# Gated linear attention and a gated layer on one core: the SyncE queue's order, another queue for one transfer, and another way to count the verdict

## The chip, the cores and the metric

The kernel runs on one core of one Trainium2 chip. A core has TensorE (PE, matrix products; its weight loads are listed as PEld), VectorE (DVE), ScalarE (ACT), GpSimd (POOL) and SyncE (SP), and sixteen DMA engines [...]. The metric is the device time of one execution in microseconds, the median of several runs. Lower is better.

## What is computed

Two blocks follow each other. The first is a recurrence with a complex gate for each of 4 x 8 heads, 768 steps, head size 48; the second takes its output as 3072 rows of 384.

```python
mag = np.sqrt(a_re * a_re + a_im * a_im)
scale = np.minimum(mag, 0.999) / (mag + 1e-06)
a_re_n, a_im_n = (a_re * scale, a_im * scale)
for t in range(S):
    new_re = ar * S_re - ai * S_im
    new_im = ar * S_im + ai * S_re
    kv = np.einsum('bhd,bhe->bhde', k[:, :, t], v[:, :, t])
    S_re, S_im = (new_re + kv, new_im)
    y[:, :, t] = np.einsum('bhd,bhde->bhe', q[:, :, t], S_re)
...
x = y.transpose(0, 2, 1, 3).reshape(3072, 384)
h = x @ w_in            # 384 x 2048
g = h * np.cos(h)
out = g @ w_out         # 2048 x 384
```

## The kernel before

**Tiling.** The 768 steps of a batch are cut into 6 chunks of 128 steps, so there are 24 chunks; two chunks make a group, and there are 12 groups (g = 0 to 11). For a group the gates become logarithms and angles (`log_steps`), whose running sums over the chunk are products on PE (`p_powers` writes the PSUM tile `lgs`, `g_phase` writes `phs`). Such a sum is taken in two halves, `hi` (copied by ACT) and `lo` (the remainder, by DVE), each with its own product. Exponentials P, Q, sine and cosine then turn keys and queries into the stacks `ks` and `qs` (`g_stack`), so that the recurrence becomes an attention inside the chunk (scores `sc`, masked by DVE into `atm`, then `yp`) and a state that goes from chunk to chunk (`sp`, then `state` on DVE).

**Transposes.** From group 2 on `ks` and `qs` are transposed with the help of DRAM (`f_transpose`, lines 921 to 939): DVE transposes blocks of 32 x 32 into `tr`, one DMA writes `tr` to `moved`, and others read it back as `kT` (four DMAs with runs of 128 bytes) and as `qT` (one DMA with runs of 2 KB). The result `yT` of a group goes through DRAM as well: two DMAs write `x` (`f_x`), and one reads it back as `xT` (`f_xt`), which is what the second block multiplies. The last row of P goes out as `row` and comes back twice as `end` (`row_out`, `row_back`); `end` is scaled in `p_end` and used by the state.

**The second block.** For each group, eight blocks `hp` multiply `xT` by `w_in`; ACT and DVE make `gate` of each. The product with `w_out` is done with seven block products instead of eight (`seventh`, lines 1160 to 1202, into the PSUM tiles `sum` and `op`), after sums of quarters of `gate` (`mixed`). ACT and DVE move the parts to `ot`, and DMAs store `ot`.

**The verdict.** The fast path holds only for gates that are not extreme. Along the way minima and maxima are collected (`least`, `odd`, `wide`), at the end `verdict` (line 1608) makes a flag of them, all engines read it, and the program branches: the general path is run if the flag is set, and otherwise the last part of the output is stored by ACT's queue. With the inputs here the flag is not set. In the version before, two columns go to DRAM (`line_d`) and come back as one row, over which DVE takes the minimum. The weights arrive as 64-bit numbers and are fetched a second time in the loop to be looked at (`guard`, DMAs to `raw` on POOL's queue, each behind the copy `after`).

**Order.** Every product on PE is chained to the one before (`matmul`, line 686), so PE's order is the order in which the program is written. That order comes from `weave` (line 1213): each list of steps is spread evenly over a stretch of the iteration, step i of a list of m over lo to hi stands at lo + (hi - lo) (i + 0.5) / m, and all steps are run by that place. The loop over n = 2 to 11 (lines 1568 to 1576) weaves the chunks of group n, the seven products of group n - 1, the `hp` blocks of group n, and the gates of group n + 1. DVE, ACT and the DMA queues are ordered by a scheduler that works from the order of writing and its estimate of times, unless `behind` sets an instruction behind another. [...] Important lists here are `chunks(n)` over 0 to 0.36,

```python
for n in range(g * G, g * G + G):
    for hh in range(2):
        yield lambda n=n, hh=hh: f_scores(n, hh)
    yield lambda n=n: f_state(n)
    yield lambda n=n: f_out(n)
yield lambda: (f_x(g), f_xt(g))
if g + 2 < NG:
    yield lambda: load(g + 2, ("k", "q", "v"))
```

`prods(n + 1)` over 0.25 to 0.27 (its first two steps are the two `lgs` sums), `products(n - 1, 0, 3)` over 0 to 0.36, and `keys(n + 1)` after the middle. The last chunk of a batch has no state to pass on, and the first has none to take.

Of the kernel before, what the change touches and what calls it, by code (L numbers as in the profile page):

```python
# [11 lines left out]
F32 = mybir.dt.float32  # L12
# [7 lines left out]
ALU = mybir.AluOpType  # L20
# [467 lines left out]
def fast_path(ctx, tc, q, k, v, a_re, a_im, moe_w_in, moe_w_out, out, least, odd, wide,  # L488
# [323 lines left out]
    def even_steps(g, i, n):  # L812


        x = X[g]
        u = cut(x["mag"], i, n)
        P, Q = cut(x["P"], i, n), cut(x["Q"], i, n)
        ins = [vector.scalar_tensor_tensor(out=u, in0=Q, scalar=HUGE, in1=P,
                                           op0=ALU.min, op1=ALU.mult)]
        yield  # L820
        for t in P, Q:
            ins.append(vector.scalar_tensor_tensor(out=t, in0=u, scalar=3.0, in1=t,
                                                   op0=ALU.subtract, op1=ALU.mult))
            yield

        for one_, what in zip(ins, ("carried", "split")):
            if what in x and g > PEG:
                behind(one_, x[what])
        if g > 0:
            row_out(g, i, n, nc.sync)  # L830
            row_back(g, i, n, nc.sync)

    def row_out(g, i, n, queue):
        P = cut(X[g]["P"], i, n)
        queue.dma_start(out=X[g]["row"][ds(i * DM, n * DM)],
                        in_=P[C - 1:C].rearrange("o x -> (o x)"))

    def row_back(g, i, n, queue):
        row = X[g]["row"][ds(i * DM, n * DM)]
        end = X[g]["end"][:, ds(i * H, n * H)]  # L840
        for a in range(2):
            queue.dma_start(out=end[ds(a * D, D)], in_=row.rearrange("(x d) -> d x", d=D))

    def p_even(g, i, n):
        for _ in even_steps(g, i, n):
# [60 lines left out]
        special(out=sn, in_=ph, func=AF.Sin, scale=TWO_PI)  # L906
        special(out=cs, in_=cs, func=AF.Sin, scale=-TWO_PI, bias=half_pi_b)

    def g_stack(g, i, n):
        x = X[g]  # L910
        if i == 0:
            for name in "ks", "qs":
                x[name] = gt.tile([C, G * H, 2, D], F32, tag=name, name=name)
        for name, product in ("ks", "Q"), ("qs", "mag"):
            for a, trig in enumerate(("cos", "sin")):
                vector.tensor_tensor(
                    out=x[name][:, ds(i * H, n * H), a],
                    in0=cut(x[product], i, n).rearrange("p (x d) -> p x d", d=D),
                    in1=cut(x[trig], i, n).rearrange("p (x d) -> p x d", d=D), op=ALU.mult)

    def f_transpose(g, i, n, name):


        if i == 0:
            X[g][name] = ft.tile([D2, G * H, Q4, 32] if name == "kT" else [D2, Q4, G * H, 32], F32,
                                 tag=name, name=name, bufs=1)
        tr = ft.tile([C, NB, n * H, 32], F32, tag="tr", name="tr")
        turn = vector.transpose(out=tr, in_=X[g][name[0] + "s"][:, ds(i * H, n * H)].rearrange(
            "p x a d -> p x (a d)").rearrange("p x (r b) -> p b x r", b=NB))
        if name == "qT" and "gated" in X[g - 1]:  # L930
            behind(turn, X[g - 1]["gated"])
        moved = rows_d.tile([Q4, D2, n * H, 32], F32, tag="moved", name="moved", bufs=3)
        nc.sync.dma_start(out=moved.rearrange("q (r b) x j -> (q r) b x j", b=NB), in_=tr)
        if name == "kT":
            for q4 in range(Q4):
                nc.sync.dma_start(out=X[g][name][:, ds(i * H, n * H), q4], in_=moved[q4])
        else:
            nc.sync.dma_start(out=X[g][name][:, :, ds(i * H, n * H)],
                              in_=moved.rearrange("q c x j -> c q x j"))

    def f_turn(g, i, name, hh):

# [217 lines left out]
    def seventh(g, p, part):  # L1160


        x, name = X[g], SEVEN[p]
        if p == 0 and part == 0:
            x["sum"] = pm.tile([C, E2], F32, tag="acc", name="sum", bufs=1)
            x["ot"] = [msb.tile([C, DM], F32, tag="ot", name="ot") for _ in range(G)]

        alone = g == NG - 1 and p == 6
        summed = p in (0, 3, 5, 6) and not alone
        if not summed and part == 0:  # L1170
            x["op"] = pm.tile([C, E2], F32, tag="m", name="op", bufs=2)
        ps = x["sum"] if summed else x["op"]
        for j in range(part * HJ // 2, (part + 1) * HJ // 2):
            matmul(ps, lhsT=left(g, name, j), rhs=right[name][:, j],
                   start=(j == 0 and (p == 0 or not summed)),
                   stop=(j == HJ - 1), skip_group_check=summed)
        if part == 0:
            return
        c11, c12, c21, c22 = (x["ot"][i][:, ts(half, E2)] for i in range(2) for half in range(2))
        if g == NG - 1:  # L1180
            c12 = rest
        if p in (0, 3, 5) or p == 6 and not alone:
            late["scalar"] = scalar.mul(out={0: c11, 3: c21, 5: c22, 6: c12}[p], in_=ps, mul=scale)
        if g == NG - 1 and p == 5:
            scalar.mul(out=c12, in_=ps, mul=scale)
        for part_ in {1: [c11], 2: [c21], 4: [c21, c22], 6: [c12] * alone}.get(p, []):
            added = vector.scalar_tensor_tensor(out=part_, in0=ps, scalar=scale,
                                                in1=part_, op0=ALU.mult, op1=ALU.add)
            if alone:
                behind(added, late["read DVE"])  # L1190
            late["vector"] = added
        row = g * G * C
        if g == NG - 1 and p == 1:
            behind(nc.sync.dma_start(out=out[ds(row, C), 0:E2], in_=c11), late["line"])
        elif p == 4:
            put = nc.sync.dma_start(out=out[ds(row + C, C), :], in_=x["ot"][1])
            if g == NG - 1:
                behind(put, late["read SP"])
        elif p == 6 and alone:
            late["store"] = lambda: nc.scalar.dma_start(out=out[ds(row, C), E2:DM], in_=c12)  # L1200
        elif p == 6:
            nc.sync.dma_start(out=out[ds(row, C), :], in_=x["ot"][0])
# [23 lines left out]
    def keys(g):  # L1226

        if not 0 <= g < NG:
            return
        for i, n in spans(g):  # L1230
            yield lambda i=i, n=n: g_trig(g, i, n)
            yield lambda i=i, n=n: (g_stack(g, i, n), p_end(g, i, n))
            for name in "kT", "qT":
                if g >= PEG:
                    yield lambda i=i, n=n, name=name: f_transpose(g, i, n, name)

    def turned(g, i, name):
        return [lambda hh=hh: f_turn(g, i, name, hh) for hh in range(2)]
# [21 lines left out]
    def chunks(g):  # L1260
        for n in range(g * G, g * G + G):
# [1 line left out]
                yield lambda n=n, hh=hh: f_scores(n, hh)  # L1263
            yield lambda n=n: f_state(n)
            yield lambda n=n: f_out(n)
        yield lambda: (f_x(g), f_xt(g))
        if g + 2 < NG:
            yield lambda: load(g + 2, ("k", "q", "v"))

    def first(g):  # L1270
        order = range(NJ // 2) if g < PLAIN else (0, 4, 1, 5, 2, 6, 3, 7)
# [296 lines left out]
    for n in range(2, NG):  # L1568
        weave((mixes(n - 1, 2, 4), 0.0, 0.12), (logs(n + 1), 0.0, 0.02), (chunks(n), 0.0, 0.36),
              (upper[2:] if n == 2 else [], 0.0, 0.2), (products(n - 1, 0, 2 + (n < NG - 1)), 0.0, 0.36),  # L1570
              (prods(n + 1), 0.25, 0.27), (second(n - 1, 1), 0.36, 0.5),
              (products(n - 1, 2 + (n < NG - 1), 7), 0.4, 0.56),
              (phases(n + 1), *((0.472, 0.476) if n == PLAIN else (0.516, 0.524))),
              (keys(n + 1), *((0.5, 0.62) if n == PLAIN else (0.53, 0.64))),
              (last_quarter() if n == PLAIN else [], 0.9, 1.0), (first(n), 0.56, 1.0),
              (mixes(n, 0, 2), 0.9, 1.0), (guarded(n - 1, per) if n > 3 else [], 0.1, 0.9))
    checked = verdict(late, temp)

    def judged():
        late["tensor"] = tail["tensor"]  # L1580
        next(checked, None)

    weave((mixes(NG - 1, 2, 4), 0.0, 0.1), ([judged], 0.05, 0.15),
          (products(NG - 1, 0, 7), 0.0, 1.0), ([judged], 0.58, 0.6), ([judged], 0.76, 0.8))
    assert not guards
    return late
@with_exitstack
def kernel(ctx, tc, q, k, v, a_re, a_im, moe_w_in, moe_w_out, out):
# [16 lines left out]
        tc.add_manual_dep(ins.ins, other.ins.name, mybir.DependencyInfo(  # L1605
            mybir.DependencyClass.NoSync, mybir.DependencyReason.DATA))

    def verdict(late, temp):

        low = keep.tile([D2, 1], F32, name="low")  # L1610
        nc.vector.tensor_reduce(out=low, in_=least, axis=AX.X, op=ALU.min)
# [4 lines left out]
        nc.vector.tensor_scalar(out=even, in0=even, scalar1=0.0, scalar2=None, op0=ALU.is_le)  # L1616
        nc.vector.tensor_scalar(out=most, in0=most, scalar1=2.4, scalar2=None, op0=ALU.is_le)
        nc.vector.tensor_tensor(out=even, in0=even, in1=most, op=ALU.mult)
        line_d = scratch.tile([D2 + C], F32, name="line_d")
        behind(nc.sync.dma_start(out=line_d[0:D2], in_=low.rearrange("p o -> (p o)")),  # L1620
               late["x"])
        nc.sync.dma_start(out=line_d[D2:D2 + C], in_=even.rearrange("p o -> (p o)"))
        line = temp("Q")[0:1, 0:D2 + C]
        late["line"] = nc.sync.dma_start(out=line, in_=line_d.unsqueeze(0))
        yield
        bad = keep.tile([1, 2], F32, name="bad")
        behind(nc.vector.tensor_reduce(out=bad[:, 0:1], in_=line, axis=AX.X, op=ALU.min),
               late["vector"])
        flag = keep.tile([1, 1], I32, name="flag")
        nc.vector.tensor_scalar(out=flag, in0=bad[:, 0:1], scalar1=0.5, scalar2=None,  # L1630
                                op0=ALU.is_lt)
        reads, values = nc.values_load_multi_w_load_instructions(
            flag[0:1, 0:1], min_val=0, max_val=1,
            skip_runtime_bounds_check_because="a comparison gives 0 or 1")
# [43 lines left out]
```

## Time and profile before

| | us |
|---|---|
| median of 3 runs | 655.68 (655.22 to 656.19) |
| the profiled execution | 653.01 |
| its span, from first to last instruction | 651.2 |
| start to the loop over n (`hp` of group 2 begins) | 154.01 |
| `hp` of group 11 begins | 607.62 |
| end of the last PE product | 646.55 |
| SP: waits for x to be written, before `xT` | 7.6 in 11 |
| DVE: `rest`, the last addition | 646.64 to 647.00 |
| the DMAs of `raw`, 768 KB each, from issue to landing | 4.6 to 5.1 |
| all DMA | 94.90 MB, 232920 packets, of which 208701 under 512 bytes |

The profile is of one execution. Its page gives the busy time of each engine and the same in 40 slices of the span; the chain that ended last is followed back from the last instruction to whatever released it. A row of the view of waits names the instruction that waited, what released it, and then the sum, the number and the longest of these waits. A row of the timeline begins with start and length in us, then engine, source line, operation, output and inputs, shape and count; what follows in brackets is how long the engine was idle before it, and for whom. One product of float32 shows as two instructions in it. Since nearly all calls go through a few helpers, the line is often a helper's (687 is `matmul`, 676 the calls on DVE and ACT), and an instruction is known by its tile.

### The profile page before, as it was taken

Reading aid. Unit: us, or ns where it says so; the run is one execution under the profiler, and the core shown is the slowest. Engines: PE = TensorE matmul, PEld = TensorE weight load, DVE = VectorE, ACT = ScalarE, POOL = GpSimd, SP = SyncE. Lnnn points to the kernel's source line nnn. Section 1 sums busy time; section 2 is a strip of 40 time slices with the busy share of each in tenths; the row PEclk is TensorE's granted clock in tenths of the full one; section 3 lists DMA queues with packets and bytes.
Section 4 is the critical chain, followed back from the end, with each engine's and each line's share of the span. In section 5 each row is a group of like instructions: output and inputs, shape, how many; then the busy total and the mean of one; then the engine's idle time right before and its main releaser. Section 6 shows DMA issues by size and latency. Waiting matters only on the chain.

```text
span 651.2 us, 10758 instructions
## 1 busy us (share of the span) xinstructions
PE 641.0 (98%) x4075; PEld 576.4 (89%) x4075; DVE 492.0 (76%) x799; ACT 392.8 (60%) x726; POOL 30.9 (5%) x53
## 2 busy tenths in 40 slices
PE   8999999999999999999999999999999999999997
PEld 6888877777999999899899899899899999999996
DVE  6999989888687688786787787876877878862251
ACT  7898687284583593494494485485576476433330
POOL 4010200000000000010010010000000000000000
PEclk9999999999999999999999999999999999999999
DMA  9968755727627656747738737836836843363001
GB/s 249 244 179 203 225 164 123 170 62 182 146 49 182 158 146 148 194 110 167 209 82 191 204 85 167 205 96 151 226 105 146 219 123 98 112 134 120 25 1 31
DMA packets 232920, 94.90 MB, mean 146 GB/s; under 512 B 208701, under 2 KB 221246, under 8 KB 232858
## 3 DMA queue, kind: packets, MB, share of 16 engines
q1 hardware_dynamic: 225320, 68.51, 45.3%
q0 software_dynamic: 5824, 25.50, 11.7%
q8 instruction: 34, 0.56, 0.4%
q10 hardware_dynamic: 1714, 0.11, 0.2%
q14 instruction: 28, 0.23, 0.1%
HBM read 69.28 MB, written 24.81 MB: 144 GB/s over the span
## 4 chain that ended last, share of the span: by engine, by line
PE 92%; ACT 4%; DVE 3%; DMA 0%; issue 0%; SPq 0%; DVEq 0%
PE hp L687 38%; PE op L687 18%; PE sum L687 16%; PE sc L687 6%; PE yp L687 6%; PE sp L687 4%; PE phs L687 2%; PE lgs L687 1%; ACT tan L707 1%; PE yr L687 1%; PE tp L948 1%; ACT rs L707 1%; ACT lg L707 1%; ACT L703 1%; DVE mag L676 1%; DVE atm L676 1%
## 5 line engine op out<-in xcount | busy, mean ns | idle before, releaser
L687 PE MATMUL hp<-xT,w_in 128*128 128x256 f32 (+1 forms) x1176 | 252.5, 375 | 0.0
L687 PEld LDWEIGHTS hp<-xT,w_in 128*128 128x128 f32 x1176 | 219.6, 190 | 30.2 <-issue 0.2
L707 ACT ACTIVATE gate<-hp,half_pi_b 128x512 f32<-128x512 f32 x96 | 66.0, 687 | 118.5 <-PE hp L687 118.5
L687 PE MATMUL op<-w_out,gate 128*128 128x192 f32 (+1 forms) x448 | 100.7, 374 | 0.0
L676 DVE TENSOR_TENSOR gate<-hp,gate 128x512 f32<-128x512 f32 x96 | 65.7, 684 | 45.8 <-ACT junk L676 45.7
L687 PEld LDWEIGHTS op<-w_out,gate 128*128 128x128 f32 x448 | 75.9, 190 | 16.9 <-issue 2.0
L676 ACT ACTIVATE junk<-hp 128x512 bf16<-128x512 f32 x96 | 56.7, 591 | 0.0
L687 PE MATMUL sum<-t_s,s 128*128 128x192 f32 x320 | 56.3, 329 | 0.0
L687 PEld LDWEIGHTS sum<-t_s,s 128*128 128x128 f32 x320 | 52.1, 190 | 1.5 <-issue 1.5
L676 DVE TENSOR_TENSOR atm<-sc,causal 128x512 f32<-128x512 f32 x48 | 32.9, 689 | 23.4 <-PE sc L687 23.4
L687 PEld LDWEIGHTS sc<-qT,kT 96*128 96x128 f32 x384 | 47.4, 192 | 2.3 <-issue 0.6
L687 PE MATMUL sc<-qT,kT 96*128 96x128 f32 x384 | 49.0, 276 | 0.2 <-ACT qT L676 0.2
L676 ACT ACTIVATE ot<-sum 128x192 f32<-128x192 f32 x39 | 12.6, 322 | 53.7 <-PE sum L687 53.4
L676 DVE SCALAR_TENSOR_TENSOR ot<-op,ot 128x192 f32<-128x192 f32 x40 | 13.3, 354 | 38.0 <-PE op L687 36.4
L687 PE MATMUL yp<-atm,v 128*48 128x128 f32 x352 | 33.6, 277 | 0.9 <-ACT Q L707 0.6
L703 ACT ACT_TABLE_LOAD x24 | 30.8, 1283 | 1.2 <-PEq L1662 0.7
L676 ACT COPY yT<-yp 48x512 f32<-48x512 f32 x44 | 25.3, 574 | 7.4 <-PE yp L687 7.0
L687 PE MATMUL yp<-qT,state 96*48 96x128 f32 x304 | 29.7, 272 | 0.0
L687 PE MATMUL sum<-w_out,gate 128*128 128x192 f32 x160 | 29.7, 329 | 0.0
L687 PE MATMUL sp<-v,ks 128*96 128x48 f32 x320 | 29.7, 245 | 0.0
L687 PEld LDWEIGHTS sp<-v,ks 128*96 128x96 f32 x320 | 29.6, 165 | 0.0
L676 ACT CAST tan<-phs 128x384 int32<-128x384 f32 x24 | 11.4, 480 | 29.4 <-PE phs L687 29.4
(147 smaller groups left out, 987.4 us busy)
## 6 DMA issues: line engine op xcount, KB each, us to landing
moved<-tr SPq DMA_DIRECT2D x20, 768.0 KB
raw<-in_moe_w_in_dram POOLq DMA_DIRECT2D x16, 768.0 KB, 5.1
raw<-in_moe_w_out_dram POOLq DMA_DIRECT2D x16, 768.0 KB, 4.6
kT<-moved SPq DMA_DIRECT2D x40, 192.0 KB
qT<-moved SPq DMA_DIRECT2D x10, 768.0 KB
k<-in_k_dram SPq DMA_DIRECT2D x24, 192.0 KB
q<-in_q_dram SPq DMA_DIRECT2D x24, 192.0 KB
v<-in_v_dram SPq DMA_DIRECT2D x24, 192.0 KB
```

The lines of the kernel that those rows point to most:

```text
L676: ins = getattr(self.engine, op)(**kw)
L687: chain(nc.tensor.matmul(out, **kw), "tensor")
L703: chain(nc.scalar.preload_act_table_set(table))
L707: chain(nc.scalar.activation(func=func, **kw))
L948: chain(nc.tensor.transpose(ps[:, h], X[g][name[0] + "s"][:, x0 + h].rearrange("p a d -> p (a d)"), ident), "tensor")
```

## The change

From group 3 on, SP's DMAs around `xT` are put in one order by hand (`there_and_back`, `in_line`): x, row, xT, the two of end, then k, q and v of the group after next, then the store of the finished chunk. The steps for xT and the loads leave the list of `chunks(n)`, and `there_and_back(n)` is woven in at 0.36. `qT` from group 3 on is read back over POOL's queue, in a chain with the fetches of `raw`, whose stretch ends at 0.68 instead of 0.9. The stack of keys is made, then transposed, then the stack of queries; `p_end` comes after both. In the last group two scalings of a PSUM tile go from ACT to DVE. The verdict is multiplied into one column, which one product with a column of ones sums on PE; the flag compares that sum with 127.5.

```diff
-        if g > 0:
+        if 0 < g <= PLAIN + 1:
             row_out(g, i, n, nc.sync)
             row_back(g, i, n, nc.sync)
+    def in_line(**kw):
+        put = nc.sync.dma_start(**kw)
+        behind(put, late["x"])
+        late["x"] = put
+
+    def there_and_back(g):
+        if g + 1 < NG:
+            row_out(g + 1, 0, G, in_line)
+        f_xt(g)
+        if g + 1 < NG:
+            row_back(g + 1, 0, G, in_line)
+        if g + 2 < NG:
+            load(g + 2, ("k", "q", "v"), put=in_line)
...
-    def g_stack(g, i, n):
+    def g_stack(g, i, n, names=("ks", "qs")):
...
-            nc.sync.dma_start(out=X[g][name][:, :, ds(i * H, n * H)],
-                              in_=moved.rearrange("q c x j -> c q x j"))
+            queue = nc.sync if g <= PEG else nc.gpsimd
+            put = queue.dma_start(out=X[g][name][:, :, ds(i * H, n * H)],
+                                  in_=moved.rearrange("q c x j -> c q x j"))
+            if g > PEG:
+                chain(put, "gpsimd")
...
-        if p in (0, 3, 5) or p == 6 and not alone:
+        if g == NG - 1 and p == 5:
+            for out_ in c22, c12:
+                vector.tensor_scalar(out=out_, in0=ps, scalar1=scale, scalar2=None, op0=ALU.mult)
+        elif p in (0, 3, 5) or p == 6 and not alone:
             late["scalar"] = scalar.mul(out={0: c11, 3: c21, 5: c22, 6: c12}[p], in_=ps, mul=scale)
-        if g == NG - 1 and p == 5:
-            scalar.mul(out=c12, in_=ps, mul=scale)
...
-            behind(nc.sync.dma_start(out=out[ds(row, C), 0:E2], in_=c11), late["line"])
+            nc.sync.dma_start(out=out[ds(row, C), 0:E2], in_=c11)
         elif p == 4:
             put = nc.sync.dma_start(out=out[ds(row + C, C), :], in_=x["ot"][1])
-            if g == NG - 1:
-                behind(put, late["read SP"])
+            behind(put, late["read SP"] if g == NG - 1 else late["x"])
...
-            yield lambda i=i, n=n: (g_stack(g, i, n), p_end(g, i, n))
+            if g <= PEG:
+                yield lambda i=i, n=n: (g_stack(g, i, n), p_end(g, i, n))
             for name in "kT", "qT":
+                if g > PEG:
+                    yield lambda i=i, n=n, name=name: g_stack(g, i, n, (name[0] + "s",))
                 if g >= PEG:
                     yield lambda i=i, n=n, name=name: f_transpose(g, i, n, name)
+            if g > PEG:
+                yield lambda i=i, n=n: p_end(g, i, n)
...
-        yield lambda: (f_x(g), f_xt(g))
-        if g + 2 < NG:
-            yield lambda: load(g + 2, ("k", "q", "v"))
+        yield lambda: f_x(g)
+        if g == PLAIN:
+            yield lambda: (f_xt(g), load(g + 2, ("k", "q", "v")))
...
-              (prods(n + 1), 0.25, 0.27), (second(n - 1, 1), 0.36, 0.5),
+              (prods(n + 1), 0.25, 0.27),
+              ([lambda: there_and_back(n)] if n > PLAIN else [], 0.36, 0.37), (second(n - 1, 1), 0.36, 0.5),
...
-              (mixes(n, 0, 2), 0.9, 1.0), (guarded(n - 1, per) if n > 3 else [], 0.1, 0.9))
-    checked = verdict(late, temp)
+              (mixes(n, 0, 2), 0.9, 1.0), (guarded(n - 1, per) if n > 3 else [], 0.1, 0.68))
+    def counted(even):
+        ps = pa.tile([1, 1], F32, tag="a", name="good")
+        matmul(ps, lhsT=even, rhs=one_b, start=True, stop=True)
+        return ps
+
+    checked = verdict(late, counted)
...
-          (products(NG - 1, 0, 7), 0.0, 1.0), ([judged], 0.58, 0.6), ([judged], 0.76, 0.8))
+          (products(NG - 1, 0, 7), 0.0, 1.0), ([judged], 0.42, 0.44), ([judged], 0.76, 0.8))
...
-        line_d = scratch.tile([D2 + C], F32, name="line_d")
-        behind(nc.sync.dma_start(out=line_d[0:D2], in_=low.rearrange("p o -> (p o)")),
-               late["x"])
-        nc.sync.dma_start(out=line_d[D2:D2 + C], in_=even.rearrange("p o -> (p o)"))
-        line = temp("Q")[0:1, 0:D2 + C]
-        late["line"] = nc.sync.dma_start(out=line, in_=line_d.unsqueeze(0))
+        nc.vector.tensor_tensor(out=even[0:D2], in0=even[0:D2], in1=low, op=ALU.mult)
         yield
-        bad = keep.tile([1, 2], F32, name="bad")
-        behind(nc.vector.tensor_reduce(out=bad[:, 0:1], in_=line, axis=AX.X, op=ALU.min),
-               late["vector"])
+        good = counted(even)
         flag = keep.tile([1, 1], I32, name="flag")
-        nc.vector.tensor_scalar(out=flag, in0=bad[:, 0:1], scalar1=0.5, scalar2=None,
-                                op0=ALU.is_lt)
+        behind(nc.vector.tensor_scalar(out=flag, in0=good, scalar1=C - 0.5, scalar2=None,
+                                       op0=ALU.is_lt), late["vector"])
```

More of the change, by code (lines that the diff above doesn't have):

```diff
@@ L828, in even_steps @@
                 behind(one_, x[what])
-        if g > 0:
+        if 0 < g <= PLAIN + 1:
             row_out(g, i, n, nc.sync)
             row_back(g, i, n, nc.sync)
+    def in_line(**kw):
[10 more added lines that the diff above has]
+            load(g + 2, ("k", "q", "v"), put=in_line)
     def row_out(g, i, n, queue):
         P = cut(X[g]["P"], i, n)
-        queue.dma_start(out=X[g]["row"][ds(i * DM, n * DM)],
-                        in_=P[C - 1:C].rearrange("o x -> (o x)"))
+        getattr(queue, "dma_start", queue)(out=X[g]["row"][ds(i * DM, n * DM)],
+                                           in_=P[C - 1:C].rearrange("o x -> (o x)"))
     def row_back(g, i, n, queue):
@@ L841, in row_back @@
         for a in range(2):
-            queue.dma_start(out=end[ds(a * D, D)], in_=row.rearrange("(x d) -> d x", d=D))
+            getattr(queue, "dma_start", queue)(out=end[ds(a * D, D)], in_=row.rearrange("(x d) -> d x", d=D))
     def p_even(g, i, n):
@@ L907, in g_trig @@
         special(out=cs, in_=cs, func=AF.Sin, scale=-TWO_PI, bias=half_pi_b)
-    def g_stack(g, i, n):
+    def g_stack(g, i, n, names=("ks", "qs")):
         x = X[g]
-        if i == 0:
-            for name in "ks", "qs":
+        for name in names:
+            product = {"ks": "Q", "qs": "mag"}[name]
+            if i == 0:
                 x[name] = gt.tile([C, G * H, 2, D], F32, tag=name, name=name)
-        for name, product in ("ks", "Q"), ("qs", "mag"):
             for a, trig in enumerate(("cos", "sin")):
@@ L1606, in behind, with verdict @@
             mybir.DependencyClass.NoSync, mybir.DependencyReason.DATA))
-    def verdict(late, temp):
+    def verdict(late, counted):
         low = keep.tile([D2, 1], F32, name="low")
```

## The prediction

> **What bounds the kernel.** I read the page first: which engine is full, and in which slices it is not.
>
> ```profile
> span 651.2 us, 10758 instructions
> PE 641.0 (98%) x4075; PEld 576.4 (89%) x4075; DVE 492.0 (76%) x799; ACT 392.8 (60%) x726; POOL 30.9 (5%) x53
> ...
> PE   8999999999999999999999999999999999999997
> ...
> DMA  9968755727627656747738737836836843363001
> ```
>
> PE is full in every slice but the first and the last, so a transfer, or work of DVE or ACT, is worth time only where PE waits for it. The view of waits says where that is. Its rows give who waited for whom, the sum in us, the times and the longest; of PE's weight loads (PEld) in the loop:
>
> ```profile
> PEld yp L687 <- issue: 2.5, 11, 0.2
> ...
> PEld op L687 <- issue: 2.0, 11, 0.2
> ...
> PEld lgs L687 <- DVE lo L676: 1.6, 4, 0.5
> ...
> PEld sum L687 <- issue: 1.5, 8, 0.2
> ```
>
> No row has PE waiting for a DMA: all that SyncE (SP) brings is there in time in this execution. The one wait for data inside the loop is that of the log sums (lgs) for lo, a DVE result. I then took the period of the loop from the chain that ended last, between the blocks "20.72 PE hp L687 x96", which begin at 154.01, 204.33, 255.53, 305.77, 356.09, 407.30, 457.54, 507.86, 559.54 and 607.62. The periods repeat with the three kinds of chunk pair: A (first of a batch; n = 3, 6, 9) 50.32, B (n = 4, 7) 51.2, C (last of a batch; n = 5, 8) 50.24. One breaks the pattern: n = 10 is of kind B and takes 51.68, 0.47 more. Its timeline beside that of n = 7 is the key to this forecast. First n = 7:
>
> ```profile
> 385.82 1.95 PE L687 MATMUL sc<-qT,kT 96*128 96x128 f32 x16
> ...
> 388.39 0.95 DVE L676 SCALAR_TENSOR_TENSOR lo<-lg,hi 128x768 fp32r<-128x768 f32 x1
> ...
> 388.91 1.48 PE L687 MATMUL sp<-v,ks 128*96 128x48 f32 x16
> ...
> 390.47 0.34 PE L687 MATMUL lgs<-lo,exact 128*128 128x384 f32 x1
> ```
>
> then n = 10:
>
> ```profile
> 537.65 1.06 PE L687 MATMUL sc<-qT,kT 96*128 96x128 f32 x8
> ...
> 540.22 0.95 DVE L676 SCALAR_TENSOR_TENSOR lo<-lg,hi 128x768 fp32r<-128x768 f32 x1
> ...
> 541.22 0.19 PEld L687 LDWEIGHTS lgs<-lo,exact 128*128 128x128 f32 x1 [0.40 <-DVE lo L676]
> ...
> 541.86 1.48 PE L687 MATMUL sp<-v,ks 128*96 128x48 f32 x16
> ```
>
> At n = 7 the sixteen state products sp stand before lgs and cover DVE's way to lo. At n = 10 they stand behind it, and PE waits 0.40.
>
> [...] at n = 10 mag and lo follow the mask product atm, which waited 0.59 for PE. [...]
>
> **The change, part by part.**
>
> SP's order. SP now issues two x, row, xT, two end, k, q, v, stores; before, row at 398.55, x 398.88, end 399.79, one k 401.21, xT 402.08, then the rest. The instructions and bytes are the same; x no longer waits behind row (31.5 us over 11 such waits of SP on DVE lg), and xT has one 192 KB load less ahead of it. PE needs xT at 407.14 in this iteration and does not wait for it. Worth 0; work of the products before it covers it. Were the cover gone, each microsecond late would cost one. Row and end now stand behind x's wait for yT; end is needed only by p_end at 410.19, end's issue was over by 401.1, and x's input yT, copied by 395.71 before, is an estimated 2 us later now (one more sum block of 1.3 and a part of the wait below ahead of it), so about 398, as before. Cost 0.
>
> qT over POOL, nine times. SP is freed of 1.19 us each (its median issue), POOL is charged 0.72 to 0.77, as for raw, of which it has 95% free. POOL's order is raw, raw, qT, after. The second raw went out at 441.18, the next qT is due near 466, and after (430.38) comes later: nothing holds it. The trace doesn't show qT's landing on POOL. From below: raw, with as many bytes, lands 4.6 to 5.1 us after issue; moved is written by about 418.3 (traffic follows the transpose's end at 415.34), so 424, with sc due at 427.64. [...] I take 0, and keep up to 1 us an iteration as the bad end (the SP form ended near 426.2, and 528.0 at n = 10, so it gains at best 0.1).
>
> Split stacks. The same four products of 0.95 and two transposes of 2.25; the transpose of ks starts one product earlier, the first gate product (412.50) has the same work ahead of it, and hp's third buffer leaves 1.7 us (first buffer free 413.17, wanted 414.9). Cost 0.
>
> Verdict. Three DMAs and a reduction (0.38) go; one DVE product of 0.15 and a 1x1 product on PE come, with its weight load 0.1 to 0.2: +0.15. It needs even, ready at 632.05, and stands near 636. The removed round trip was over with flag at 642.27, while the end hangs on the last PE product, rest at 646.64 and the final store: no gain. The two scalings that move from ACT to DVE (0.33, 0.32) land in DVE gaps of 1.7 us and more: 0.
>
> The unasked part: the weave. chunks(n) loses its tenth item, the load. Ten items over 0 to 0.36 stood 0.036 apart, nine stand 0.04 apart. The second state product (index 6) was at 6.5 x 0.036 = 0.234, before the log sums at 0.252; now it is at 0.26, behind them. So n = 3 to 9 get the PE order of n = 10, which never had the load. PE is chained by hand, so this order is certain. Prices:
> - B, n = 4 and 7: DVE's order is that of n = 10 too. 0.40 each: 0.8.
> - C, n = 5 and 8: no second state product, and lgs waited 0.45 already. 0.
> - A, n = 3, 6, 9: here DVE's new order is atm, ot, mag, lo, with ot (0.35) ahead. ot waits for the op block that PE runs 0.89 to 2.36 after sc (as 538.54 to 540.01 against 537.65). At n = 6 sc begins at 334.61: op ends 336.97, ot ends 337.36, mag 338.2, lo 339.1. PE is ready for lo at about 3.3 after sc, 337.9: a wait of 1.2. Or from n = 10: lo comes 1.02 later than there, 0.40 + 1.02 = 1.42. I take 1.3 each: 3.9, kept between 1.15 and 1.42. ACT's hi shifts by one yT copy (0.58) to 337.76 and is not last.
>
> Sum: 3.9 + 0.8 + 0.15 = +4.85 (4.3 to 5.3). PE has no slack after lgs to take it back. Profiled execution: 653.01 (span 651.2 and 1.8 around) becomes 657.9. The median of the runs is 655.68, 2.67 above the profiled one; I add to that: **660.5**.
>
> **Rivals.**
> 1. *Relief.* The 2.67 may be late transfers in unprofiled runs, which the new SP order mends. For it: qT's traffic ends 1.4 before use. Against: no PE wait on DMA. Time: 655.68 - 2.67 + 4.85 = 657.9.
> 2. *Not slower: late xT at the hand-over.* The same mechanism, but larger: if unprofiled runs lose more than 4.85 / 9 = 0.54 us at each of nine hand-overs from yT to xT, the new order outweighs the waits. At 0.7 each: 655.68 - 6.3 + 4.85 = 654.2. It needs more than the 2.67 that can be seen between the executions.
> 3. *lo in time.* If the new DVE order costs nothing because lo's inputs come earlier, only the product remains: 655.8. Against: n = 10, where lo wasn't in time.
> 4. *qT late on POOL.* 1 us in nine iterations: 669.5 with the waits.
>
> **How the numbers follow.** Forecast 0.58 (own range 659.9 to 661.2), relief 0.18, not slower 0.15, lo in time 0.05, qT late 0.04. Forecast, relief and a part of the rest make 0.8: 656.6 to 662.0. A measurement of this kernel can tell about 0.2%, 1.3 us, from no change. Slower by more: forecast, relief and late qT, 0.80, less 0.03 for relief beyond what I grant it: 0.77. Within: 0.07. Faster: 0.16.
>
> **What would show it.** In the changed profile, the row of weight loads of lgs waiting for DVE lo should grow from 1.6 in 4 to about 6.3 in 9 (3.9 and 0.8 new, 0.9 at C, 0.4 at n = 10, 0.3 at the start), with 1.1 to 1.4 at n = 3, 6, 9; the periods A and B should read 51.6 and 51.6, C 50.2; the tail from the last hp block the same to 0.2. A new PE wait of sc for qT, or of hp for xT, would speak for rival 4 or a failed queue; periods of 50.3 and 51.2 with a smaller gap to the median would refute me.

## The result, and the profile after

The changed kernel takes 664.57 us on the median of 4 runs (664.14 to 664.94), the kernel before 655.93 beside it (655.22 to 656.41): ratio 1.0136, 95% interval 1.0121 to 1.0151, so it is 8.6 us slower. The profiled execution is 664.25 us, with a span of 662.4. That span is 11.2 more than in the profile of before, whose execution lay 2.67 below its median; the trace therefore shows more loss than the medians do.

First the page of the changed kernel: span, busy time of the engines, and the part on DMA queues (packets, MB, time of the packets as a share of 16 engines' span).

```profile
span 662.4 us, 10764 instructions
PE 644.2 (97%) x4077; PEld 576.4 (87%) x4077; DVE 493.2 (74%) x801; ACT 392.6 (59%) x724; POOL 40.3 (6%) x62
...
q1 hardware_dynamic: 221462, 61.43, 48.8%
q0 software_dynamic: 7696, 32.57, 16.9%
```

The same part of the page of before:

```profile
q1 hardware_dynamic: 225320, 68.51, 45.3%
q0 software_dynamic: 5824, 25.50, 11.7%
```

q1 is SyncE's queue, q0 GpSimd's. qT's 7.1 MB have gone from one to the other, as they should. But the two shares together went from 57.0 to 65.7%, for the same 94.9 MB and 1% fewer packets, over a longer span. Moving the same bytes took more packets' time than before. Nothing in the diff asks for that, and it turned out to be the key.

The view of waits of the changed kernel, weight loads (PEld) and then products (PE):

```profile
PEld lgs L687 <- DVE lo L676: 5.7, 9, 1.1
PEld sc L687 <- issue: 4.7, 9, 1.6
PEld sc L687 <- DMA qT<-moved: 3.7, 3, 1.9
```

```profile
PE sc L687 <- DMA kT<-moved: 3.8, 4, 1.6
PE lgs L687 <- DVE lo L676: 2.8, 4, 0.9
```

The first row is the wait that was forecast (1.6 in 4 before). The next rows for sc are new: the first scores of an iteration wait for kT or qT. Before, no row had sc waiting for a DMA; its longest row was this:

```profile
PEld sc L687 <- issue: 0.6, 3, 0.3
```

("issue" in the PEld row only says that the profile names no releaser; the same waits have one in the view of the products.) The timeline at n = 3 shows the forecast wait itself:

```profile
185.92 0.83 ACT L728 ACTIVATE hi<-lg 128x768 fp32r<-128x768 f32 x1
...
187.13 0.95 DVE L676 SCALAR_TENSOR_TENSOR lo<-lg,hi 128x768 fp32r<-128x768 f32 x1
...
188.13 0.19 PEld L687 LDWEIGHTS lgs<-lo,exact 128*128 128x128 f32 x1 [1.15 <-DVE lo L676]
...
188.59 0.51 PEld L687 LDWEIGHTS sp<-v,ks 128*96 128x96 f32 x4
```

The second state product sp, which used to stand ahead of lgs, now stands behind it.

The two losses can be told apart by iteration. The table is worked out from the traces: time from the first scores of iteration n to the start of its hp block, and from there to the first scores of n + 1 (20.72 when PE waits for nothing).

| n | 3 | 4 | 5 | 6 | 7 | 8 | 9 | 10 |
|---|---|---|---|---|---|---|---|---|
| scores to hp, before | 29.60 | 30.49 | 29.52 | 29.60 | 30.49 | 29.51 | 29.60 | 30.90 |
| scores to hp, after | 30.96 | 30.88 | 29.54 | 30.99 | 30.92 | 29.53 | 30.98 | 30.91 |
| hp to scores, before | 20.72 | 20.72 | 20.72 | 20.72 | 20.72 | 20.72 | 20.79 | 20.72 |
| hp to scores, after | 20.72 | 22.45 | 21.39 | 20.93 | 21.62 | 20.77 | 22.17 | 21.38 |

The upper pair is the weave: 1.36, 1.39 and 1.38 at n = 3, 6, 9, 0.39 and 0.43 at n = 4, 7, nothing at n = 5, 8, 10; together 4.95 us. The lower pair is the hand-over of kT and qT: 5.6 us that nobody had asked for, with another 0.8 up to the scores of n = 2.

### The profile page after: what moved, and what is told of

It is laid out like the page before. It is cut to its first block, busy times and chain, and to the rows that moved or that the text cites. A ratio compares the mean times of both kernels' runs of the same rounds, so it can differ in the third digit from the quotient of the medians.

```text
span 662.4 us, 10764 instructions
## 1 busy us (share of the span) xinstructions
PE 644.2 (97%) x4077; PEld 576.4 (87%) x4077; DVE 493.2 (74%) x801; ACT 392.6 (59%) x724; POOL 40.3 (6%) x62
## 4 chain that ended last, share of the span: by engine, by line
PE 76%; DVE 9%; DMA 7%; ACT 4%; SPq 3%; issue 2%; POOL 0%; DVEq 0%
PE hp L687 25%; PE op L687 17%; PE sum L687 14%; PE yp L687 5%; PE sc L687 5%; DMA kT<-moved 5%; PE sp L687 4%; SPq L951 3%; DVE tr L676 2%; PE phs L687 2%; PE lgs L687 1%; DVE mag L676 1%; DVE lo L676 1%; DVE ks L676 1%; DVE tan L676 1%
## 5 line engine op out<-in xcount | busy, mean ns | idle before, releaser
L687 PE MATMUL sum<-t_s,s 128*128 128x192 f32 x320 | 57.8, 330 | 0.0
L687 PE MATMUL sc<-qT,kT 96*128 96x128 f32 x384 | 50.8, 277 | 4.9 <-DMA kT<-moved 3.8
```

What stands on the lines that cost most here:

```text
L687: chain(nc.tensor.matmul(out, **kw), "tensor")
```

## The experiments

Theories at the start: *weave* (lgs ahead of sp) and *queue* (qT on GpSimd's queue and kT on SyncE's hold each other up, and both come late); against *queue*, that SyncE's new order, or the split stacks, make kT late. Runs marked "in before", and the four that take one part of the change each, edit the kernel before; the others edit the changed one. All times below are medians, and each ratio is the one found with its interval from the runs side by side, not the quotient of the medians; in the four series the kernel before took 654.66, 654.67, 654.49 and 655.33 beside them.

### Undoing the weave, the queue, both; and the queue alone

```
 def chunks(g):                      # e1_order, e3_both
     if g == PLAIN: ...
+    elif g + 2 < NG:
+        yield lambda: None
 def f_transpose(...)                # e2_qt_sync, e3_both: after; e4_before_pool: the reverse, in before
-    queue = nc.sync if g <= PEG else nc.gpsimd
+    queue = nc.sync
```

> The changed kernel with one empty tenth item put back into chunks(n) for n = 3 to 9, so that TensorE's order in the loop is that of the kernel before (the second state product ahead of the log sums again); queues, split stacks and verdict stay changed. Before 655.9, after 664.6 on the median. Two causes (the order of the weave, and qT that lands late for the scores from GpSimd's queue): the waits of lgs for lo shrink from 5.7 in 9 to about 1.6 in 4 in the row of weight loads, the waits of the scores for kT and qT stay: 660.3 (659.5 to 661.2). Order alone (the late scores are only a sequel of it): 656.0. Order worth nothing, the new SP sequence or qT's queue is all: 664.5.

> The changed kernel with qT written from SyncE's queue again, all else changed, the order of the weave too. Two causes: the scores' waits for kT and qT (8 in the sum of PE's weight loads and products over the iterations) go, those of lgs stay: 659.8 (658 to 660.8), near the forecast of 660.5. Rival, SyncE's new order (k, q, v loads and stores moved behind xT) makes moved and kT late whoever issues qT: no gain, 664 to 665. Order alone: 664.5 too, since the late scores would remain.

> The changed kernel with both undone: the empty tenth item in chunks and qT from SyncE's queue. What is left of the change is SyncE's new order, the split stacks, and the verdict by a product. Two causes: 655.5 (654 to 656.3), with no waits of lgs at n = 3 to 9 apart from C's 0.4 and no waits of the scores for kT or qT. If the hand-over from yT to xT gained something in unprofiled runs, below 654.5. Rival, SyncE's new order makes kT late: 659 to 661.

> The kernel before with nothing but qT written from GpSimd's queue for groups 3 to 11; SyncE's order, stacks, weave and verdict as before. Two causes: the scores wait for kT and qT as in the changed kernel, 4 to 5 in the median: 660.2 (658.5 to 661.5). Rival, SyncE's new order is what makes them late: 655.7 (655 to 656.5). Rival, only the order and the queue together do it (less time is left between stack and scores): 656 to 658.

| run | us | ratio to before | packets' time of the two queues |
|---|---|---|---|
| e1_order | 660.36 | 1.0085 (1.0067 to 1.0104) | 48.6 + 17.0% |
| e2_qt_sync | 663.75 | 1.0138 (1.0122 to 1.0155) | 54.1 + 11.8% |
| e3_both | 657.25 | 1.0039 (1.0024 to 1.0055) | 53.9 + 11.9% |
| e4_before_pool | 664.40 | 1.0167 (1.0140 to 1.0194) | 41.0 + 15.3% |

The first met its number for two causes, though the second cause will turn out to be another than the queue. The second run missed its number: with qT back on SyncE nothing was gained. Its trace holds a new wait, of the sums for ACT:

```profile
PE sum L687 <- ACT ot L676: 4.7, 4, 1.7
```

With qT on SyncE the scheduler places ACT's copies to ot and DVE's gate products otherwise, so this run changed more than a queue and can't price it. The third, with both undone, was expected at 655.5 and was still 2.6 slower than before: a third cause. The fourth, expected at 660.2, lost more than *queue* alone could explain. Two things stood out. The packets' time is near 66% in every version of the changed kernel, whichever queue carries qT, and below 57% in the fourth, so the queue doesn't set it. And in the fourth, GpSimd's queue held a second transfer right behind qT (timeline):

```profile
268.11 0.69 POOL L939 DMA_DIRECT2D qT<-moved  x1 [38.81 <-DMA moved<-tr]
...
268.80 0.76 POOL L629 DMA_DIRECT2D raw<-in_moe_w_in_dram  x1
```

In the changed kernel raw isn't there: the diff also shortens the stretch of `guarded` from 0.1 to 0.9 to 0.1 to 0.68.

### Each part of the change alone, in the kernel before

s5_pool68 is e4_before_pool with that second edit; the other three take one part of the diff each.

```
-  (guarded(n - 1, per) if n > 3 else [], 0.1, 0.9)        # s5_pool68, with qT on GpSimd
+  (guarded(n - 1, per) if n > 3 else [], 0.1, 0.68)
+  ([lambda: there_and_back(n)] if n > PLAIN else [], 0.36, 0.37)   # s1_sp, with in_line, row_out,
+  elif g + 2 < NG: yield lambda: None                     #   behind(put, late["x"]) and the empty item
-  checked = verdict(late, temp)                           # s2_verdict, with counted, the 1x1 product,
+  checked = verdict(late, counted)                        #   and c12, c22 scaled on VectorE
+  def g_stack(g, i, n, names=("ks", "qs"))                # s3_split, with the new order in keys
```

> The kernel before with qT of groups 3 to 11 written from GpSimd's queue, as in the run that added this alone, and with the second edit that the changed kernel has beside it: the weight pieces (raw) are placed in 0.1 to 0.68 of an iteration, not 0.1 to 0.9, so that the second raw leaves 13 us after the first scores and not right behind qT. Times against 654.7 for the kernel before. If raw behind qT, 768 KB more in the same stretch, made most of the 9.7 us of that run: 657.8 (656.8 to 658.8), the 3.1 by which the two runs with the old weave differed over qT's queue. [...] If qT from GpSimd costs nothing and SyncE's new order is the cause: 654.7.

> The kernel before with SyncE's new order alone (x, row, xT, ends, loads, stores chained by hand; qT from SyncE, stacks, verdict as before; an empty item keeps the old weave). The run with the weave and qT's queue undone was still 2.6 over the kernel before. If SyncE's order carries that: 657.3, with the scores waiting for kT or qT at three or four hand-overs, and with the packets' time of SyncE's queue at 53 to 54% of 16 engines' span, not 45%. If the split stacks or the verdict carry it: 654.7 and 45%.

> The kernel before with the verdict's part alone: counted by a product with ones, the three DMAs gone, the two last scalings on VectorE. The forecast's price of 0.15: 654.8. If the end of the kernel gains by the round trip taken away: 653.5 to 654.4. If the DMAs taken away shift something that slows the transfers of the loop: 656 to 657.5.

> The kernel before with the split stacks alone: ks stacked and transposed before qs is stacked, p_end behind both. The forecast's price of 0: 654.7. If the second stack behind the first transpose makes moved and kT late by what VectorE puts between: 655.5 to 657.5, with waits of the scores at the hand-overs.

| run | us | ratio to before | packets' time of the two queues |
|---|---|---|---|
| s5_pool68 | 653.76 | 0.9989 (0.9978 to 1.0001) | 41.6 + 15.6% |
| s1_sp | 656.11 | 1.0018 (1.0009 to 1.0027) | 45.4 + 11.6% |
| s2_verdict | 658.02 | 1.0047 (1.0033 to 1.0061) | 53.1 + 11.9% |
| s3_split | 654.45 | 0.9995 (0.9984 to 1.0005) | 45.3 + 11.7% |

So the queue theory fell: qT over GpSimd costs nothing where raw is out of its way. raw right behind qT cost about 11 us in the other run (10.6 between the medians, 11.7 by the ratios), with DVE's and ACT's work on raw moved along with it. The split stacks cost nothing. SyncE's order alone costs 1.4, between its two numbers, and only in part by late transfers (scores waiting for qT, 0.7 us in the trace): packets' time is as before. The scheduler chose another order for DVE with it, and PE now waits for masked scores; first the row before, then that of s1_sp:

```profile
PE yp L687 <- DVE atm L676: 0.3, 1, 0.3
PE yp L687 <- DVE atm L676: 1.8, 6, 0.4
```

The surprise is the verdict. It acts at the end of the kernel, but its version loses 3.3 us (more than any of its expectations), by its trace nearly all of it in the loop, and the packets' time of SyncE's queue jumps from 45.3 to 53.1%, though TensorE has the order of before but for the one product at the end. What of it can act in the loop? The tiles of the program. The verdict's edit also removes the tile `bad` (8 bytes a partition) from the pool `keep`, whose tiles lie in SBUF. In the compiled program its slot is 32 bytes, and all that is allocated behind it moves down by 32: k from 75136 to 75104, kT from 121344 to 121312. The tiles that the loop's DMAs touch (re, im, k, q, v, tr, kT, qT, yT, xT, ot, end, raw) stood at multiples of 64 in the kernel before; none of them does after. (`line_d`, the tile in DRAM that went too, was the last one there; no DRAM address of the loop changed.)

### Addresses alone

```
+  keep.tile([1, 2], F32, name="pad")      # p1_after_pad, p4_order_pad: 8 bytes, unused
+  keep.tile([1, 120], F32, name="pad")    # p2_before_off32: 480 bytes, in before
+  keep.tile([1, 112], F32, name="pad")    # p3_before_off64: 448 bytes, in before
   flag = keep.tile([1, 1], I32, name="flag")
+  elif g + 2 < NG: yield lambda: None     # p4_order_pad too, in chunks
```

> The changed kernel with one unused tile of 8 bytes a partition put into the pool keep where bad was, so that every tile allocated behind it stands at the SBUF address it has in the kernel before; the instructions and their order on every engine are those of the changed kernel. The theory: bad's slot of 32 bytes went with the verdict's edit, all later tiles moved down by 32 (k from 75136 to 75104, kT from 121344 to 121312), off multiples of 64, and transfers of short runs take longer. Then the packets' time of SyncE's and GpSimd's queues falls from 65.7% of 16 engines' span to about 57%, the scores' waits for kT and qT go, the weave's 4.7 to 5 and up to 1.4 of SyncE's order stay: 660.0 (659 to 661), against 654.7 before. Rival, the addresses don't matter and the product or the order in VectorE's queue does: 663.5 to 664.6, packets' time unchanged.

> The kernel before with an unused tile of 480 bytes in the pool keep and nothing else: same instructions in the same order, the tiles behind it stand at addresses that are congruent to those of the changed kernel (32 below a multiple of 64; the same remainder by 512). If the addresses alone make the 3.3 of the run with the verdict alone: 658.0 (657 to 658.6), packets' time of SyncE's queue at 53%, the scores waiting at two or three hand-overs. Rival, something else of the verdict's edit: 654.7 and 45%.

> The kernel before with an unused tile of 448 bytes there: the tiles stand 64 below a multiple of 128, so still at multiples of 64. If a multiple of 64 is what counts: 654.7, packets' time of SyncE's queue 45 to 46%. [...]

> The changed kernel with the addresses restored as in the first run of this call and with the empty item that restores the weave. What is left: SyncE's order, qT over GpSimd, split stacks, verdict by a product, all at the old addresses. If weave and addresses are the whole loss: 654.7 to 655.5, perhaps 653.8 if qT's queue gives back what it did alone. Rival, SyncE's order costs the 1.4 that it cost alone: 656.1.

| run | us | ratio to before | packets' time of the two queues |
|---|---|---|---|
| p1_after_pad | 658.51 | 1.0061 (1.0047 to 1.0076) | 41.8 + 15.6% |
| p2_before_off32 | 657.88 | 1.0047 (1.0034 to 1.0061) | 53.0 + 11.7% |
| p3_before_off64 | 656.44 | 1.0041 (1.0024 to 1.0059) | 49.9 + 11.7% |
| p4_order_pad | 652.84 | 0.9974 (0.9966 to 0.9983) | 41.9 + 15.6% |

p2 is the clean proof: the kernel before with an unused tile, every engine's instructions in the same order, has the whole loss of the verdict's edit and the same packets' time, for the same packets and bytes. From its page:

```profile
q1 hardware_dynamic: 225320, 68.51, 53.0%
```

There is a second such pair: e1_order and p4_order_pad have the same instructions in the same order on every engine and differ in the addresses alone, and their ratios are 1.0085 and 0.9974. The hand-over of p2 beside that of before, by windows of 2 us from the start of kT's transfers to the first scores (length, then busy time of PE, PEld, DVE, ACT and POOL, PE's clock, packets' time as a share of the 16 DMA engines, and GB/s; the share passes 1 where packets overlap, of which up to 30 are under way at once in the trace of before). Before, with the scores at 276.09:

```profile
266.09:268.09 2.00, 2.00 (x11) 1.76 (x10) 0.95 (x3) 1.17 (x3) 0.00 (x0) 1.00 1.12 201
268.09:270.09 2.00, 2.00 (x11) 1.75 (x10) 1.77 (x5) 1.27 (x3) 0.00 (x0) 1.00 1.09 173
...
272.09:274.09 2.00, 2.00 (x11) 1.77 (x10) 1.61 (x4) 0.68 (x3) 0.00 (x0) 1.00 1.01 296
274.09:276.09 2.00, 2.00 (x12) 1.74 (x10) 1.29 (x3) 0.88 (x3) 0.00 (x0) 1.00 0.17 48
```

p2_before_off32, with the scores at 278.79:

```profile
268.79:270.79 2.00, 2.00 (x11) 1.77 (x10) 1.93 (x5) 0.83 (x2) 0.00 (x0) 1.00 1.46 171
270.79:272.79 2.00, 2.00 (x11) 1.74 (x11) 0.96 (x2) 0.68 (x3) 0.00 (x0) 1.00 1.59 127
...
274.79:276.79 2.00, 2.00 (x11) 1.77 (x10) 1.65 (x5) 1.26 (x3) 0.00 (x0) 1.00 1.04 279
276.79:278.79 2.00, 0.90 (x6) 0.48 (x4) 0.34 (x1) 1.06 (x3) 0.00 (x0) 1.00 0.34 80
```

While kT is brought in (runs of 128 bytes), the packets of p2 take more time (1.46 and 1.59 against 1.12 and 1.09) and move less (171 and 127 GB/s against 201 and 173). qT's runs of 2 KB follow at nearly the old rate (279 against 296). kT thus ends later, qT after it, and in the last window PE stands still for 1.1 us.

p1 is the changed kernel with nothing but its addresses restored. It came out 0.5 us below its expected range (659 to 661), and the scores no longer wait for kT or qT; of the two losses only lgs is left in the view of waits:

```profile
PEld lgs L687 <- DVE lo L676: 6.1, 9, 1.5
PEld lgs L687 <- DVE lg L676: 1.3, 2, 0.7
```

p4 restores the weave as well and is faster than the kernel before, and 1 us below the lowest number expected of it. It has neither SyncE's 1.4 (with qT on GpSimd, ACT's order in the loop is that of before) nor a wait for a transfer.

### The granule, the weave alone, and a better version

```
+  keep.tile([1, 32], F32, name="pad")                  # q1_off128: 128 bytes, in before
-  yield lambda: (f_x(g), f_xt(g))                      # w1_weave, in before
-  if g + 2 < NG:
-      yield lambda: load(g + 2, ("k", "q", "v"))
+  yield lambda: (f_x(g), f_xt(g), g + 2 < NG and load(g + 2, ("k", "q", "v")))
+  elif g < NG - 1: yield lambda: None                  # q2_best: after, with the pad of 8 bytes
```

> The kernel before with an unused tile of 128 bytes in the pool keep: kT, qT, tr and the others stand 128 past a multiple of 512. If a multiple of 128 is enough: 654.5, packets' time of SyncE's queue at 45 to 46%. If the start must be a multiple of 256 or 512: 655.5 to 657, 48 to 50%, as with the shift of 64 (49.9%).

> The kernel before with the load of k, q, v put into the item before it, so that chunks(n) has nine items for n = 3 to 9: TensorE's order in the loop becomes that of the changed kernel, SyncE's order, queues, stacks, verdict and addresses stay. The forecast's step alone: 654.5 + 4.7 = 659.2. By the traces, 1.31 at each A and 0.35 at each B: 654.5 + 4.6 = 659.1. By the difference of the two runs with restored addresses: 654.5 + 5.7 = 660.2. Nothing, if the lgs wait is made up elsewhere: 654.5.

> The changed kernel with restored addresses and the empty tenth item for n = 3 to 10, so that lgs stands behind the second state product in the last full iteration too. Against the run without n = 10 (0.9974 of the kernel before, 652.8): its wait of 0.40 at n = 10 goes, 652.4. Rival, the other items that move at n = 10 (sum blocks, DVE's ot) cost as much: 652.8 to 653.2.

| run | us | ratio to before | packets' time of the two queues |
|---|---|---|---|
| q1_off128 | 656.00 | 1.0007 (0.9995 to 1.0018) | 46.1 + 12.0% |
| w1_weave | 659.83 | 1.0071 (1.0049 to 1.0093) | 45.1 + 11.8% |
| q2_best | 652.75 | 0.9961 (0.9940 to 0.9982) | 41.8 + 16.0% |

With kT 128 past a multiple of 512 next to nothing is lost (packets' time of 46.1%, next to the 45 to 46 expected if 128 is enough; the median is 0.7 above that of before, but the ratio's interval holds 1). With kT 64 below one the packets' time grows by 4.6 points, with kT 32 below one by 7.7. In the time of the kernel the last two can't be told apart. The weave alone costs 0.71% of 655.33, 4.65 us, as forecast. So the 5.7 between p4 and p1 hold about 1 us more than the weave. The profiled executions of p1 and w1 show one candidate: at n = 9 the scores-to-hp stretch takes 33.14 and 34.78 us in them, where 30.91 is the weave's, with DVE held 1.45 in both by a late raw ahead of lg and lo. How often this happens in other executions isn't known.

q2_best has the old order at n = 10 too, and that period is 51.20 in its trace, not 51.56 as in p4. In the timed runs the two can't be told apart. Both beat the kernel before.

## Why the prediction was wrong, point by point

**The failed step is the verdict's price.** The prediction counted its instructions ("+0.15") and was right on those; the tail from the last hp block to the end takes 43.35 us, 43.6 before. What it didn't count is what the edit takes out of memory: the tile `bad`, and with it the alignment of nearly all tiles of the loop. Alone this costs 3.3 to 3.4 us (s2, p2). In the whole change it is the step from p1 to after: ratio 1.0061 to 1.0136, some 4.9 us (worked out over the ratios, since the two ran beside different runs of before). With the weave undone it is larger: from p4 to e1, 0.9974 to 1.0085, some 7.3.

**The weave** was right in mechanism, place and size: 4.70 forecast; 4.95 in the table, 4.65 alone. n = 3, 6, 9 lost 1.36 to 1.39 (forecast 1.3), n = 4 and 7 0.39 and 0.43 (0.40), n = 5 and 8 nothing (0). The row of lgs was to be 6.3 in 9; it is 5.7 in 9. The periods of 51.6 and 51.6 for A and B and 50.2 for C were hidden in the changed kernel by the new waits; with the old addresses (p1) they read 51.63, 51.55 and 50.16 at n = 3, 4 and 5.

**qT over POOL**, taken as 0 with a bad end of 1 us an iteration: 0 is right (s5, 0.9989). The landing was thought to be that of raw, 4.6 to 5.1; it is 6.4 at the old addresses beside kT and 7.3 at the new ones. The new waits of the scores look like rival 4, which was to be shown by just such a wait. They are not: they are there with qT on either queue if the addresses are off (e1 on GpSimd, e3 and p2 on SyncE), and at the old addresses they are gone (p4, before) or small (0.7 us in s1), but for e4 with its raw behind qT. The two do add up: at the new addresses qT on GpSimd takes 3.1 more than on SyncE (e1 and e3), though DVE and ACT differ between those two as well.

**SyncE's order**, priced at 0, costs 1.4 alone. By the waits of its trace most of that comes through the order that the scheduler then gives DVE and ACT, which the prediction took as unmoved; no run changed that order by itself. In the changed kernel with the weave and the addresses undone (p4) this cost doesn't appear. **Split stacks**, 0: right.

**The 2.67 between median and profile** was carried over whole. Rival 1 held that late transfers make it and the new order mends them. p4 speaks for a part of that: its 14 runs lie between 652.59 and 654.12, those of before beside them between 652.90 and 656.52. A trace with the instructions of before (q1) does show one hp block waiting for xT, at n = 8, in this view of the products:

```profile
PE hp L687 <- DMA xT<-x: 1.6, 1, 1.6
```

and p4's shows none. One such trace is not a proof that this is what the 2.67 is made of, and s5, which leaves SyncE's order alone but for qT, is also a little lower; the share of each stays open.

Put together by ratios, each step with the one before it: before to p4 -0.26%, the weave (p4 to p1) +0.87%, the addresses (p1 to after) +0.75%; sum 1.36%. Without the addresses the change would stand at 655.68 x 1.0061 = 659.7, against the forecast of 660.5. That these lie so close is in part luck: the rest of the change gains 1.7 us (p4), which no term of the forecast's sum held, and the step from p4 to p1 costs about 1 us more than the weave alone.

## What to carry to other kernels

An edit also changes where things lie: compare the addresses of the tiles before and after, not only the instructions, especially when a small tile goes or comes in a pool that others are stacked on. Here the sign of it was a share of packets' time that rose while bytes and packets didn't, and an unused tile that puts the addresses back was a cheap test. And the name on a wait (qT, on the queue that was just changed) is not its cause; only the runs that had the one without the other could tell.

## What the runs showed of the hardware

In these runs the start of a tile in SBUF changed how long its transfers with short runs took. The kernel before, same instructions, tiles moved by an unused one (kT's address stands for the shift of all; the others start at other remainders, k for instance 384 past a multiple of 512 in the kernel before):

| kT starts at | above or below a multiple of 512 | packets' time of SyncE's queue | ratio to before |
|---|---|---|---|
| 121344 | 0 | 45.3% | 1 |
| 121472 | 128 above | 46.1% | 1.0007 (0.9995 to 1.0018) |
| 121792 | 64 below | 49.9% | 1.0041 (1.0024 to 1.0059) |
| 121824 | 32 below | 53.0% | 1.0047 (1.0034 to 1.0061) |

The packets kept in the traces tell which transfers pay. In SyncE's queue the packets of 128 bytes are those of kT (61440 of them, together kT's 40 transfers of 192 KB), and those of 192 bytes are the loads of re, im, k, q and v (122880). Both read DRAM, whose addresses didn't move, and write SBUF. The mean time of one packet in ns, worked out from the four traces:

| packets | kT at 0 | 128 above | 64 below | 32 below |
|---|---|---|---|---|
| 128 bytes (kT) | 13.0 | 13.0 | 19.3 | 18.9 |
| 192 bytes (the loads) | 15.6 | 15.9 | 15.8 | 18.5 |

So the shift by 64 slows the packets of kT but not the loads, and the shift by 32 slows both, which is why it has the larger share of packets' time. The median packet takes 13 and 15 ns in all four; it is a part of the packets that takes much longer (of kT's, one in twenty takes 42 ns or more at 32 below, and 13 before). The packets of 6144 bytes from `tr` to `moved`, which read SBUF, change little (253 ns before, 260 at 32 below). In the changed kernel the means are 18.2 and 19.4, with its addresses restored (p1) 13.4 and 16.1.

kT's shifted side is the one that is written. Why a write that starts there takes longer was not shown, and neither was what makes a start a good one: kT's packets took 13.0 ns at the two starts that are multiples of 128, and 19.3 and 18.9 ns at the two that are not, but four starts leave room for other explanations.

A second transfer of 768 KB right behind qT on GpSimd's queue cost about 11 us over nine iterations (e4 against s5), though the bytes of the kernel are the same. In e4's trace, measured as in the table by iteration, some 8 us stand at the hand-over, where the scores wait for kT (6.5 in 6 by the view of waits). Whether the transfers slow each other there was not shown, since the work of DVE and ACT on raw moved too.
